# A batch-one attention-and-MLP decode kernel: 128 rows of w2 loaded by five GpSimd loads on chosen partitions, and GpSimd opening the first part

## The chip, the cores and the metric

The kernel runs on one core of a Trainium2 chip. A core has a matmul engine (TensorE, PE in the profile), VectorE (DVE), ScalarE (ACT), GpSimd (POOL) and SyncE (SP), an on-chip memory of 128 partitions (SBUF), accumulators for the matmuls (PSUM), and 16 DMA engines that bring data from HBM. The engines run their own instruction queues and wait for each other by semaphores. A load is issued by an instruction on some engine's queue (here nearly always SP's), cut into packets, and carried by the DMA engines.

The metric is the device time of one execution in microseconds (us). It was measured twice for the kernel before: 400.61 and 400.65, median 400.63. One more execution was taken under the profiler; it has its own time.

## The reference

One token (batch 1, sequence 1) of width 1024 goes through two branches that are added to it:

```python
xn = _layernorm(x)                       # x: [1, 1, 1024]
return x + A_ref(xn, k_cache, v_cache, wq, wo) + B_ref(xn, w1, w2, w3, w4)

# A_ref: q = xn @ wq            wq [1024, 4096], 32 heads of 128
#        scores against k_cache [1, 4, 65536, 128], softmax, times v_cache, 8 query heads per cache head
#        result @ wo            wo [4096, 1024]
# B_ref: h  = gelu(layernorm(xn) @ w1)                    w1 [1024, 1024]
#        hs = concat(four quarters of h, each shifted along the sequence, zeros shifted in) @ w2
#        x1 = xn + hs                                     w2 [1024, 1024]
#        x1 + gelu(layernorm(x1) @ w3) @ w4               w3 [1024, 3584], w4 [3584, 1024]
```

All is bfloat16 in memory. The sequence has length 1, so every shift by one or two places moves zeros in: the row that meets w2 is all zeros whatever h is, and x1 equals xn. The weights and caches together are 169.87 MB, of which the two caches are 134 MB.

## The kernel before

**Staging.** Three large buffers in SBUF (`slot0` to `slot2`, 128 partitions of 64 KB each) take turns. A list called `stream` gives the order: wq, w3, w1 and w2 together ("w12"), then for each of eight units a K tile and a V tile of 8 MB, then wo, then w4. Item n goes to slot n mod 3. Each load spreads its rows over the 128 partitions in order, so that partition m holds the m-th block of rows; a whole slot is 128 rows of 64 KB. w2 is loaded as 8 rows (16 KB) per partition by one load (line 296). All these loads are issued on SP's queue (`prog.load("sp", ...)`, line 89), in the order of the list. When the computation that reads an item has been written, `freed` (line 311) writes down the load of the item three places later; that load waits for the last matmul that reads the slot.

**Recording and waits.** The kernel doesn't call the engines directly. A small layer (`Program`) records every operation with the regions it reads and writes (`region`, line 26), and `plan` (line 124) then works out which operation must wait for which, by overlap of regions. Two operations that touch the same columns on overlapping ranges of partitions are ordered; operations on GpSimd always wait for the GpSimd operation before them (line 151). Each load has a semaphore of its own, raised as it lands. `mm` (line 95) records a matmul and, where the weights at its place in the array aren't those already held, a weight load (LDWEIGHTS). A row times a matrix is done with `row_acc` (line 342): the row's piece, one column of 128 values, is broadcast to 32 columns, and the matmul adds to a 32-partition strip of the accumulator `psB`; strips 0 and 32 take the two 512-wide halves.

**Order.** The load of wq stands in a first part of its own, ahead of everything else (`tile_critical`, line 574, whose opening and closing are done by SP). After it come x_row's load on ACT's queue, w3 and w12 on SP's, and on GpSimd a run of memsets and copies that make constants (lines 325 to 340). Then: the two layer norms; `compute_wq` (q, transposed and written into `qdiag` by GpSimd, line 412); `compute_w3` (gelu, kept in `hT` to the end); `compute_w12` (line 430): 16 matmuls with w1, a gelu, and 16 matmuls of `g_col` with w2, where `g_col` is the row of zeros of the reference. Each of the eight units then transposes its K tile in four DVE instructions, multiplies it with the queries in 64 matmuls (`sc`), finds the maximum, takes the exponential on ACT, transposes the weights on DVE, and multiplies them with V in 64 matmuls (`oacc`). At the end come wo (64 matmuls), and w4 in five loads of 8, 12, 5, 2 and 1 rows per partition (line 19), the last rows in narrow matmuls; two casts and a store by ACT's queue finish.

Of the kernel before, what the change touches and what calls it, by code (L numbers as in the profile page):

```python
# [7 lines left out]
BF16 = mybir.dt.bfloat16  # L8
F32 = mybir.dt.float32
# [5 lines left out]
P = 128  # L15
ROW = 32768
# [3 lines left out]
NARROW = 8  # L20
AHEAD = 5

WIDTH = {F32: 4, BF16: 2}


def region(ap):

    dims, size = list(ap.ap), WIDTH[ap.dtype]
    pitch, rows = dims[0]
    at = ap.offset % pitch  # L30
    last = at + sum((n - 1) * s for s, n in dims[1:])
    p0 = ap.offset // pitch
    return ap.tensor.name, p0, p0 + rows, at * size, (last + 1) * size


def meet(a, b):
    return a[0] == b[0] and a[1] < b[2] and b[1] < a[2] and a[3] < b[4] and b[3] < a[4]


class Op:  # L40
    def __init__(self, engine, emit, reads, writes, alone=False, transfer=False):
        self.engine, self.emit, self.alone, self.transfer = engine, emit, alone, transfer
        self.reads = [region(a) for a in reads]
        self.writes = [region(a) for a in writes]
        self.waits = []
        self.awaited = False


class Program:
# [45 lines left out]
    def mm(self, out, lhsT, rhs, start, stop, pos=(0, 0), size=(P, P)):  # L95

        pe, nc = self.engines["pe"], self.nc
        what = (str(lhsT), size)
        if any(s != size for (_, s), _ in self.held.values()):
            self.held.clear()  # L100
        if pos not in self.held or self.held[pos][0] != what:
            self.add(Op("pe", lambda: pe.ldweights(lhsT, tile_position=pos), [lhsT], []))  # L102
            self.held[pos] = (what, region(lhsT))

        def emit():
            return pe.add_instruction(mybir.InstMatmult(  # L106
                name=nc.get_next_instruction_name(), engine=mybir.EngineType.PE, start_tensor_calc=start,
                stop_tensor_calc=stop, tile_size=size, tile_position=pos, ldweights=False, bass_skip_group_check=True,
                ins=[pe.lower_ap(rhs), pe.lower_ap(lhsT)], outs=[pe.lower_ap(out)]))
        return self.add(Op("pe", emit, [rhs, lhsT], [out]))  # L110
# [13 lines left out]
    def plan(self):  # L124

        known = {e: {} for e in self.engines}
        count = {e: 0 for e in self.engines}
        writers, readers, last_pool = {}, {}, None
        for n, op in enumerate(self.ops):
            e, op.n = op.engine, n  # L130
            need = {}

            def needs(other, raw):
                if other.queue == e and (e in self.IN_ORDER or not raw):
                    return
                if known[e].get(other.queue, 0) < other.at:
                    if other.queue not in need or need[other.queue].at < other.at:
                        need[other.queue] = other

            for r in op.reads:  # L140
                for region_, other in writers.get(r[0], ()):
                    if meet(r, region_):
                        needs(other, True)
            for w in op.writes:
                for region_, other in writers.get(w[0], ()):
                    if meet(w, region_):
                        needs(other, True)
                for region_, other in readers.get(w[0], ()):
                    if meet(w, region_):
                        needs(other, False)  # L150
            if e == "pool" and last_pool is not None:
                needs(last_pool, True)
            picked = sorted(need.values(), key=lambda o: o.n)
            kept = [o for o in picked
                    if not any(o is not x and x.clock.get(o.queue, 0) >= o.at for x in picked)]
            for o in kept:
                o.awaited = True
                for q, at in o.clock.items():
                    known[e][q] = max(known[e].get(q, 0), at)
            op.waits = kept  # L160
            if op.transfer:
                op.queue, op.at = ("dma", n), 1
            else:
                count[e] += 1
                op.queue, op.at = e, count[e]
            if e == "pool":
                last_pool = op
            op.clock = dict(known[e])
            op.clock[op.queue] = op.at
            for w in op.writes:  # L170
                for table in (writers, readers):
                    kept_ = [(r, o) for r, o in table.get(w[0], ())
                             if not (w[1] <= r[1] and r[2] <= w[2] and w[3] <= r[3] and r[4] <= w[4])]
                    table[w[0]] = kept_
                writers[w[0]].append((w, op))
            for r in op.reads:
                readers.setdefault(r[0], []).append((r, op))
# [29 lines left out]
def kernel(  # L207
# [15 lines left out]
    D = A_x.shape[-1]  # L223
# [6 lines left out]
    DC = D // P  # L230
    FC = F // P
    UKEYS = P * ROW // DH
    assert DH == P and HQ // HKV == 8 and HKV == 4 and D == 1024 and F == 3584 and S == 1
    assert SK == 2 * UKEYS and sum(W4_PIECES) == FC
    NB = 2
    NU = HKV * NB
    SCALE = float(DH) ** -0.5
    LEAD = 8 * (SETS - 1)
    COLS = (P, 32)

    prog = Program(nc)
    pe, dve, act, pool = prog, prog.dve, prog.act, prog.pool
# [17 lines left out]
    g_col = sb("g_col", [P, 1], BF16)  # L260
# [14 lines left out]
    sc = ps("sc", [P, SUBS, 512])  # L275
    oacc = ps("oacc", [P, 512])
    pm = [ps(f"pm{i}", [P, 512]) for i in range(2)]
    psB = ps("psB", [P, 512])
# [7 lines left out]
    tiles = {it: slots[i % 3] for i, it in enumerate(stream)}  # L286

    def load(it):
        t = tiles[it]
        if it == "wq":  # L290
            prog.load("sp", t[:], A_wq.rearrange("(p c) n -> p (c n)", c=DC))
        elif it == "w3":
            prog.load("sp", t[:, 0:DC * F], B_w3.rearrange("(p c) f -> p (c f)", c=DC))
        elif it == "w12":
            prog.load("sp", t[:, 0:DC * D], B_w1.rearrange("(p c) n -> p (c n)", c=DC))
            prog.load("sp", t[:, DC * D:2 * DC * D], B_w2.rearrange("(m c) n -> m (c n)", c=DC))
        elif it == "wo":
            prog.load("sp", t[:], A_wo.rearrange("(p j) n -> p (j n)", p=P))
        elif it == "w4":
            w4_v = B_w4.rearrange("(m c) n -> m c n", c=FC)  # L300
            c0 = 0
            for n in W4_PIECES:
                prog.load("sp", t[:, c0 * D:(c0 + n) * D], w4_v[:, c0:c0 + n, :].rearrange("p c n -> p (c n)"))
                c0 += n
        else:
            kind, i = it
            g, b = divmod(i, NB)
            cache = A_k_cache if kind == "K" else A_v_cache
            prog.load("sp", t[:], cache[0, g, b * UKEYS:(b + 1) * UKEYS, :].rearrange("(p ct) d -> p (ct d)", p=P))
# [10 lines left out]
    dve.memset(x_row[:], 0.0)  # L320
    prog.load("act", x_row[0:1, :], A_x[0, 0:1, :])
    load("w3")
    load("w12")

    pool.memset(ident_f[:], 0.0)
    pool.affine_select(out=ident_f[:], in_=ident_f[:], compare_op=ALU.not_equal, fill=1.0, base=0,
# [11 lines left out]
    pool.memset(x_halves[:], 0.0)  # L338
    pool.memset(qdiag[:], 0.0)
    pool.memset(g_col[:], 0.0)  # L340

    def row_acc(j, lhsT, rhs, start=False):
        return pe.mm(psB[32 * j:32 * j + 32, :], lhsT.to_broadcast([P, 32]), rhs, start, False, (0, 32 * j), COLS)

    x_t = p_sb[:, 0:DC * 32].rearrange("p (c j) -> p c j", j=32)
    for a in range(4):
# [29 lines left out]
    _, xn2_rep, _, _ = layernorm(xn, "b")  # L376
# [51 lines left out]
        dve.tensor_copy(out=hT[:], in_=h_row[:, ::32])  # L428

    def compute_w12():  # L430
        wt = tiles["w12"][:, 0:2 * DC * D].rearrange("p (w c n) -> p w c n", w=2, c=DC)
        for c in range(DC):
            for q in range(2):
                pe.mm(sc[0:32, q, :], xn2_rep[:, c, :], wt[:, 0, c, 512 * q:512 * (q + 1)], c == 0, c == DC - 1,
                      (0, 0), COLS)
        h1 = p_sb[0:32, 0:1024].rearrange("p (q n) -> p q n", q=2)
        act.activation(out=h1, in_=sc[0:32, 0:2, :], func=ACTF.Gelu_apprx_tanh)
        for c in range(DC):
            for j in range(2):
                row_acc(j, g_col[:], wt[:, 1, c, 512 * j:512 * (j + 1)], start=(c == 0))  # L440
        freed("w12")

    W = ROW // SETS

    nball = [sb(f"nball{i}", [P, NB]) for i in range(2)]
    lall = [sb(f"lall{i}", [P, NB]) for i in range(2)]
    mx = sb("mx", [P, 1])
    m8 = sb("m8", [1, 8])
    rep = sb("rep", [1, P])
    negmg = sb("negmg", [P, 1])  # L450
    wb = sb("wb", [P, NB])
    lw = sb("lw", [P, NB])
    rl = sb("rl", [P, 1])
# [73 lines left out]
    for u in range(NU):  # L527
        g, b = divmod(u, NB)
# [18 lines left out]
    wt = tiles["w4"]  # L547
# [23 lines left out]
    store = prog.store("act", out[0, 0, :].rearrange("(j n) -> j n", j=2), out_t[31:33].rearrange("p h n -> p (h n)"))  # L571

    prog.plan()
    with tc.tile_critical(sync_engine=mybir.EngineType.SP, no_gpsimd_drain=True):
        prog.emit(0, opening)
    tc.close()
    tc.compile()
# [39 lines left out]
```

## Time and profile before

| | |
|---|---|
| median of the two timed runs | 400.63 us (400.61 to 400.65) |
| the profiled execution, its own time | 400.47 us |
| its span, first to last instruction | 399.2 us |
| busy: PE / DVE / ACT / POOL | 223.5 / 210.2 / 27.6 / 6.2 us |
| loads on SP's and ACT's queues | 3744 packets on SP's, 169.87 MB |
| mean rate over the span | 426 GB/s |
| instructions in the trace: TensorE (with weight loads) | 2250, of 2557 in all |

The page gives busy time and idle time per engine, a picture of the span in 40 slices with the DMA engines' share, the DMA queues with their packets, and a chain: the work that ended last, followed back to what released it. The queues named there are q1 (SP's loads), q10 (ACT's), q8 ("instruction": blocks of 16 KB that the trace shows in 9 packets), and q14 (tables). "SPq" means the queue of SP, which issues a load; a load's duration there is the issue, not the transfer. A load's landing is seen in the trace as 16 marks on its semaphore, and the packets as 16 parallel rows of back-to-back packets; the trace gives packets a queue and times, not the number of their DMA engine.

### The profile page before, as it was taken

How to read it: one execution, taken by the hardware profiler on the slowest of the kernel's cores; microseconds unless marked ns; L12 is line 12 of the kernel's file. 1: busy time of each engine (PE TensorE's matmuls, PEld its weight loads, DVE VectorE, ACT ScalarE, POOL GpSimd, SP SyncE). 2: the span in 40 equal slices, each digit the busy share in tenths (PEclk: the TensorE clock that was granted, in tenths of full speed). 3: DMA queues.
4: the chain of work that ended last, by engine and by line, in shares of the span. 5: the costliest groups of instructions: out<-in, count | busy, mean ns of one | idle time of the engine just before them, and what ended most of it. 6: DMA issues, size and time to landing. Idle time of an engine off the chain costs nothing.

```text
span 399.2 us, 2557 instructions
## 1 busy us (share of the span) xinstructions
PE 223.5 (56%) x1360; PEld 45.8 (11%) x890; DVE 210.2 (53%) x156; ACT 27.6 (7%) x35; POOL 6.2 (2%) x29
## 2 busy tenths in 40 slices
PE   0260970592469256923874196529652946393687
PEld 0210010010100020001001000201020102000233
DVE  0521010975096549653963795259439942793411
ACT  1010030002000200020002000200010011002000
POOL 2000000000000000000000000000000000000000
PEclk9995795598869666978796889568867995698669
DMA  8989999999999999999999999999999999999996
GB/s 329 506 374 419 470 420 427 421 453 479 415 420 427 420 429 427 460 460 420 415 427 420 440 427 455 453 420 420 427 429 440 427 460 435 420 420 427 402 439 259
DMA packets 3760, 170.03 MB, mean 426 GB/s; under 512 B 419, under 2 KB 421, under 8 KB 678
## 3 DMA queue, kind: packets, MB, share of 16 engines
q1 hardware_dynamic: 3744, 169.87, 98.7%
q8 instruction: 9, 0.15, 0.1%
q14 instruction: 1, 0.01, 0.0%
q10 hardware_dynamic: 6, 0.00, 0.0%
HBM read 169.87 MB, written 0.00 MB: 426 GB/s over the span
## 4 chain that ended last, share of the span: by engine, by line
DMA 56%; DVE 24%; PE 14%; another core or an unknown queue 2%; ACT 2%; issue 0%; SPq 0%
DMA slot<-in_A_k_cache_dram 42%; DVE slot L82 19%; PE sc L106 9%; DMA slot<-in_B_w_dram 9%; DMA slot<-in_A_wq_dram 5%; PE oacc L106 4%; DVE p_sb L82 2%; DVE mx L82 2%; ACT p_sb L82 2%; PE pm L122 1%; DVE m L82 0%; DVE rep L82 0%; DVE nball L82 0%; DVE x_halves L82 0%
## 5 line engine op out<-in xcount | busy, mean ns | idle before, releaser
L82 DVE STREAM_TRANSPOSE slot<-slot 128x4096 f32<-128x4096 f32 x32 | 139.4, 4411 | 52.2 <-DMA slot<-in_A_k_cache_dram 52.2
L106 PE MATMUL sc<-slot,qdiag 128*128 128x512 bf16 x512 | 128.2, 410 | 69.0 <-DVE slot L82 68.9
L106 PE MATMUL oacc<-slot,p_sb 128*32 128x512 bf16 x512 | 46.3, 542 | 37.5 <-DVE p_sb L82 18.7
L82 DVE STREAM_TRANSPOSE p_sb<-p_sb 128x2048 bf16<-128x2048 bf16 (+2 forms) x10 | 20.8, 2084 | 38.4 <-ACT p_sb L82 38.3
L82 DVE TENSOR_REDUCE mx<-sc 128x1 f32<-128x2048 f32 x8 | 18.3, 2291 | 29.7 <-PE sc L106 29.7
L102 PEld LDWEIGHTS <-qdiag 128*128 128x128 bf16 x128 | 13.0, 102 | 180.0 <-issue 180.0
L82 ACT ACTIVATE p_sb<-sc,nball 128x2048 bf16<-128x2048 f32 x8 | 15.7, 1967 | 249.9 <-DVE nball L82 249.9
L102 PEld LDWEIGHTS <-p_sb 128*32 128x32 bf16 x512 | 17.3, 131 | 63.3 <-issue 21.8
L106 PE MATMUL sc<-slot,ln_rep_b 128*32 128x512 bf16 (+1 forms) x80 | 16.2, 832 | 8.8 <-DMA slot<-in_B_w_dram 8.6
L82 DVE SCALAR_TENSOR_TENSOR og<-oacc,wb,og 128x512 f32<-128x512 f32 x4 | 3.0, 750 | 19.9 <-PE oacc L106 19.9
L122 PE MATMUL pm<-ident_f,mx 128*1 128x128 f32 x8 | 2.3, 283 | 19.1 <-DVE mx L82 19.1
L106 PE MATMUL psB<-slot,oT 128*32 128x512 bf16 x64 | 9.3, 463 | 1.3 <-DVE oT L82 1.3
L116 PE MATMUL pm<-ol,selx 128*128 128x129 f32 x8 | 2.6, 414 | 10.6 <-DVE ol L82 10.6
L106 PE MATMUL sc<-slot,ln_rep_a 128*32 128x512 bf16 x64 | 6.0, 559 | 4.2 <-DMA slot<-in_A_wq_dram 4.2
L116 PE MATMUL pm<-ln_rowsum_a,msk 128*128 128x1 f32 x2 | 0.6, 363 | 13.5 <-DVE ln_rowsum_a L82 13.5
L82 DVE TENSOR_TENSOR og<-psB,slot 64x512 f32<-64x512 f32 x1 | 0.7, 683 | 13.2 <-PE psB L106 13.2
L82 POOL COPY qdiag<-qx 32x32 bf16<-32x32 bf16 x16 | 3.2, 202 | 277.2 <-PE sc L106 250.5
L82 DVE STREAM_TRANSPOSE p_sb<-x_row 32x256 bf16<-32x256 bf16 x4 | 2.5, 616 | 7.6 <-DMA x_row<-in_A_x_dram 7.6
L122 PE MATMUL pm<-ident_f,rep 1*128 1x1 f32 x8 | 1.9, 235 | 5.0 <-DVE rep L82 5.0
L82 ACT COPY og<-oacc 128x512 f32<-128x512 f32 x4 | 2.3, 585 | 32.9 <-PE oacc L106 32.9
L82 DVE CAST p_sb<-sc 128x512 bf16<-128x512 f32 x1 | 0.7, 691 | 7.4 <-PE sc L106 7.4
L106 PE MATMUL psB<-slot,hT 128*32 128x512 bf16 x40 | 4.5, 379 | 0.0
(86 smaller groups left out, 63.1 us busy)
## 6 DMA issues: line engine op xcount, KB each, us to landing
slot<-in_B_w_dram SPq DMA_DIRECT2D x1, 7168.0 KB, 37.4
slot<-in_B_w_dram SPq DMA_DIRECT2D x3, 2048.0 KB, 43.4
slot<-in_B_w_dram SPq DMA_DIRECT2D x1, 3072.0 KB, 34.5
slot<-in_B_w_dram SPq DMA_DIRECT2D x1, 1280.0 KB, 33.5
slot<-in_B_w_dram SPq DMA_DIRECT2D x1, 512.0 KB, 34.4
slot<-in_B_w_dram SPq DMA_DIRECT2D x1, 256.0 KB, 34.5
slot<-in_A_k_cache_dram SPq DMA_DIRECT2D x8, 42.1
slot<-in_A_v_cache_dram SPq DMA_DIRECT2D x8, 36.9
```

The costliest lines, as they stand in the source:

```text
L82: return program.add(Op(engine, lambda: method(*args, **kw), reads, writes, alone=kw.get("accum_out") is not None))
L102: self.add(Op("pe", lambda: pe.ldweights(lhsT, tile_position=pos), [lhsT], []))
L106: return pe.add_instruction(mybir.InstMatmult(name=nc.get_next_instruction_name(), engine=mybir.EngineType.PE, start_tensor_calc=start, st ...
L116: return self.add(Op("pe", lambda: pe.matmul(out, lhsT=lhsT, rhs=rhs, start=start, stop=stop, tile_position=pos, skip_group_check=True), [ ...
L122: return self.add(Op("pe", lambda: pe.transpose(out, in_, identity), [in_, identity], [out]))
```

## The change

Three things are changed.

- w2's load on SP's queue takes 7 rows per partition instead of 8 (896 rows). The other 128 rows are loaded by five loads on GpSimd's queue, onto 16 chosen partitions: 4 partitions of 17 rows, 2 of 9, 2 of 1, 2 of 17 and 6 of 1. A row is 2 KB. The columns behind the 7 rows are set to zero on partitions 0 to 63 first, by a GpSimd memset of 64 x 8704 float32, since most of them receive fewer than 17 rows. `load("w12")` moves behind GpSimd's memsets in the text.
- `compute_w12` has 14 matmuls over the 7 rows and 34 over the 17 columns of extra rows, the latter on 64 partitions (a tile of 64 x 32).
- The first part is opened and closed by GpSimd instead of SP.

`regions` replaces `region`, so that a load on every fourth partition is known row by row; and a GpSimd load is no longer the operation that the next GpSimd operation waits for.

```diff
+W2_ROWS = 7
+W2_EXTRA = ((0, 4, 4, 17), (1, 4, 2, 9), (2, 4, 2, 1), (16, 4, 2, 17), (24, 4, 6, 1))
...
-def region(ap):
+def regions(ap):
     dims, size = list(ap.ap), WIDTH[ap.dtype]
-    pitch, rows = dims[0]
+    stride, rows = dims[0]
+    pitch = ROW * WIDTH[BF16] // size if ap.tensor.name.startswith("slot") else stride
     at = ap.offset % pitch
     last = at + sum((n - 1) * s for s, n in dims[1:])
     p0 = ap.offset // pitch
-    return ap.tensor.name, p0, p0 + rows, at * size, (last + 1) * size
+    if rows > 1 and stride > pitch:
+        parts = [(p0 + i * (stride // pitch), p0 + i * (stride // pitch) + 1) for i in range(rows)]
+    else:
+        parts = [(p0, p0 + rows)]
+    return [(ap.tensor.name, a, b, at * size, (last + 1) * size) for a, b in parts]
...
-            if e == "pool":
+            if e == "pool" and not op.transfer:
                 last_pool = op
...
-            prog.load("sp", t[:, DC * D:2 * DC * D], B_w2.rearrange("(m c) n -> m (c n)", c=DC))
+            prog.load("sp", t[:, DC * D:W2_REST], B_w2[0:P * W2_ROWS, :].rearrange("(m c) n -> m (c n)", c=W2_ROWS))
+            k0 = P * W2_ROWS
+            for p0, step, k, c in W2_EXTRA:
+                prog.load("pool", t[p0:p0 + step * k:step, W2_REST:W2_REST + c * D],
+                          B_w2[k0:k0 + k * c, :].rearrange("(m c) n -> m (c n)", c=c))
+                k0 += k * c
...
     load("w3")
-    load("w12")
...
     pool.memset(g_col[:], 0.0)
-
-    def row_acc(j, lhsT, rhs, start=False):
-        return pe.mm(psB[32 * j:32 * j + 32, :], lhsT.to_broadcast([P, 32]), rhs, start, False, (0, 32 * j), COLS)
+    more = max(c for _, _, _, c in W2_EXTRA)
+    pool.memset(tiles["w12"][0:64, W2_REST:W2_REST + more * D].bitcast(F32), 0.0)
+    load("w12")
+
+    def row_acc(j, lhsT, rhs, start=False, k=P):
+        return pe.mm(psB[32 * j:32 * j + 32, :], lhsT.to_broadcast([k, 32]), rhs, start, False, (0, 32 * j), (k, 32))
...
-        for c in range(DC):
+        for c in range(W2_ROWS):
             for j in range(2):
-                row_acc(j, g_col[:], wt[:, 1, c, 512 * j:512 * (j + 1)], start=(c == 0))
+                row_acc(j, g_col[:], wt[:, D * (DC + c) + 512 * j:D * (DC + c) + 512 * (j + 1)], start=(c == 0))
+        for c in range(more):
+            for j in range(2):
+                row_acc(j, g_col[0:64, :], wt[0:64, W2_REST + D * c + 512 * j:W2_REST + D * c + 512 * (j + 1)], k=64)
...
-    with tc.tile_critical(sync_engine=mybir.EngineType.SP, no_gpsimd_drain=True):
+    with tc.tile_critical(sync_engine=mybir.EngineType.Pool, no_gpsimd_drain=True):
```

More of the change, by code (lines that the diff above doesn't have):

```diff
@@ L42, in __init__ @@
         self.engine, self.emit, self.alone, self.transfer = engine, emit, alone, transfer
-        self.reads = [region(a) for a in reads]
-        self.writes = [region(a) for a in writes]
+        self.reads = [r for a in reads for r in regions(a)]
+        self.writes = [r for a in writes for r in regions(a)]
         self.waits = []
@@ L102, in mm @@
             self.add(Op("pe", lambda: pe.ldweights(lhsT, tile_position=pos), [lhsT], []))
-            self.held[pos] = (what, region(lhsT))
+            self.held[pos] = (what, regions(lhsT)[0])
         def emit():
@@ L234 @@
     assert SK == 2 * UKEYS and sum(W4_PIECES) == FC
+    W2_REST = (DC + W2_ROWS) * D
     NB = 2
@@ L295, in load @@
             prog.load("sp", t[:, 0:DC * D], B_w1.rearrange("(p c) n -> p (c n)", c=DC))
-            prog.load("sp", t[:, DC * D:2 * DC * D], B_w2.rearrange("(m c) n -> m (c n)", c=DC))
+            prog.load("sp", t[:, DC * D:W2_REST], B_w2[0:P * W2_ROWS, :].rearrange("(m c) n -> m (c n)", c=W2_ROWS))
[4 more added lines that the diff above has]
+                k0 += k * c
+            assert k0 == D
         elif it == "wo":
@@ L430, in compute_w12 @@
     def compute_w12():
-        wt = tiles["w12"][:, 0:2 * DC * D].rearrange("p (w c n) -> p w c n", w=2, c=DC)
+        wt = tiles["w12"]
         for c in range(DC):
             for q in range(2):
-                pe.mm(sc[0:32, q, :], xn2_rep[:, c, :], wt[:, 0, c, 512 * q:512 * (q + 1)], c == 0, c == DC - 1,
+                pe.mm(sc[0:32, q, :], xn2_rep[:, c, :], wt[:, D * c + 512 * q:D * c + 512 * (q + 1)], c == 0, c == DC - 1,
                       (0, 0), COLS)
```

## The prediction

> **What bounds the kernel now.** I read the picture in 40 slices and the table of DMA queues first. The columns of the queue table are packets, MB, and the time the packets took as a share of 16 engines' span.
>
> ```profile
> DMA  8989999999999999999999999999999999999996
> GB/s 329 506 374 419 470 420 427 421 453 479 415 420 427 420 429 427 460 460 420 415 427 420 440 427 455 453 420 420 427 429 440 427 460 435 420 420 427 402 439 259
> q1 hardware_dynamic: 3744, 169.87, 98.7%
> q8 instruction: 9, 0.15, 0.1%
> ```
>
> The DMA engines are busy from the second slice to the last, 98.7% of the span with SP's loads alone, while PE has 56% and DVE 53%. So the time is set by how long 16 DMA engines take for their share, and then by the tail behind the last load. The chain of waits, in order of time, ends so (start, duration, what):
>
> ```profile
> 341.29 17.43 DVE slot L82 x4
> ...
> 362.62 34.50 DMA slot<-in_B_w_dram
> 397.12 0.04 issue
> 397.16 0.34 PE pm L106 x4
> 397.50 0.02 issue
> 397.53 0.43 DVE x_halves L82
> ```
>
> The last w4 load is done at 397.12 and 2.1 us of matmuls, casts and store follow to 399.2. A second path runs close beside it: the last K tile lands at 341.27, and from there DVE and PE work with little pause to 395.13, when the sums with wo and most of w4 end; the narrow matmuls then wait 0.17 and 0.22 us for their loads. So an earlier last load alone gains at most some 0.2 us before PE is late instead (PE is through with what it had at 396.94); only if the last K tile comes earlier as well does the whole end move.
>
> A bulk load ends with its slowest engine. Every load leaves 16 landing marks, one per DMA engine. wq's final packets end within 0.36 us of each other (22.03 to 22.39). The K tile that is in at 127.76 already has a spread of 1.75 us, and from 166 us on it is 1.9 us. Behind the first of the 16, those of w4's first load stand at 0, 0, 0.02, 0.04, 0.07 | 0.30, 0.31 | 0.99 | 1.53, 1.61, 1.63, 1.69, 1.69, 1.70, 1.70, 1.90 us. **Eight engines of sixteen are late by 1.5 us or more.** The trace tells why: the number of late engines rises by one after each q8 packet. The window 396.0 to 397.2 shows one such packet alone (same columns):
>
> ```profile
> q1 hardware_dynamic: 49, 0.08, 17.9%
> q8 instruction: 1, 0.02, 5.5%
> ```
>
> 5.5% of 16 x 1.2 us is 1.05 us for 16 KB, and one engine carries no load meanwhile. After the fetch at 104.44 the next 64 KB packet of that engine also takes 2.89 instead of 2.42 us, so a fetch puts an engine back by 1.05 + 0.47 = some 1.5 us. Eight fetches lie at 43.99, 104.44, 145.74, 198.76, 246.96, 297.93, 338.97 and 377.68, each on another engine; a table load at 75.28 makes the one at 0.99. The ninth, at 396.52, comes too late to hurt. Perfectly even engines would end at the mean of these marks, 0.95 instead of 1.90: about 0.95 us is all that balance can bring.
>
> [...]
>
> **The change part by part.** *Bytes per engine.* The bulk w2 load loses 2 KB on each partition, 8 partitions per engine: 16 KB, by the rate of the 64 KB packets (65,536 B in 2.42 us, 27.1 GB/s) 0.60 us less on every engine. The extra rows come back as 16 shares, one per chosen partition: 17 rows 1.29 us, 9 rows 0.68, 1 row 0.08. If each share has an engine of its own, six engines get 0.68 us more, two 0.08 more, eight 0.53 less. The store, two partitions, shows two packets and x_row, one partition, one packet, so a share per partition is what the trace has for small transfers; it doesn't show on which engine GpSimd's shares come to lie. There are as many light shares (eight) as late engines. With light on late, the late ones come to at most 1.90 - 0.53 = 1.37, the one at 0.99 with a middle share to 1.07, the six fast ones to 0.68 to 0.99: **-0.53 us** at every load from the first K tile on, the last K tile and the last w4 load alike, so both paths move.
>
> *Foreign packets on the engines.* Each engine now carries one GpSimd share between SP's packets. x_row's 2 KB packet on ACT's queue held its engine's next packet back by 0.08 us, which is its bytes: no switching cost. The nearest dear rows are the 16 KB fetch (0.9 us above its bytes) and the 8 KB table load (0.7 above). So 0 to +0.9 us on all 16 alike; I take **+0.1**, nearest to x_row, which like the shares goes from HBM to SBUF.
>
> *The ninth fetch.* PE gains 32 matmuls, 2 weight loads and 2 instructions for waits on five loads; blocks of instructions are therefore used up 36 instructions earlier after w2. The fetches 2 to 8 move by some 1 to 12 us, which changes nothing in their sum. The ninth falls in a dense stretch (80 PE instructions in 4.5 us, 390.65 to 395.13) and comes at about 394.5 to 395.4, while w4's last pieces are still on their way. Its engine loses 1.05 us (packets are small there, so hardly the 0.47). On one that was fast and has a middle share it ends at 0 to 0.31, plus 0.08 and 1.05: 1.13 to 1.44, not far from the 1.28 of the late ones (the last load's slowest mark is 1.81, less 0.53). I take **+0.05** for this.
>
> *GpSimd's queue.* The new memset has 8704 columns; the rows of 536 columns in 0.54 us and of 128 in 0.20 give 1.0 to 1.6 ns each, 8.7 to 14 us. GpSimd is free at 5.57 us, so the memset ends by 14.3 to 19.5, then five issues (SP's take 0.33, ACT's 0.53; even 2 us each would end before 30). The next GpSimd work is the copy of the queries, which began at 31.54, and PE needs that only at 57.8. Cover for either is over 10 us; w2's extra rows are needed by PE at about 57. A share ahead of wq's last packets lets wq land up to 1.3 us later, which moves the wq stage; K's first load was issued at 28.84, while w3 and w12 keep the queue full to 49: hidden. SP's own queue keeps its order, and no load on it waits for GpSimd.
>
> *PE in the w2 stage.* 32 matmuls at 0.21 us (6 in 1.24 on the timeline) are 6.7 us.
>
> ```profile
> 56.64 1.24 PE L106 MATMUL psB<-slot,g_col 128*32 128x512 bf16 x6
> 57.81 0.10 PEld L102 LDWEIGHTS <-qdiag 128*128 128x128 bf16 x1 [1.94 <-issue]
> 57.92 0.33 SPq L89 DMA_DIRECT2D slot<-in_A_k_cache_dram  x1
> 70.17 17.42 DVE L82 STREAM_TRANSPOSE slot<-slot 128x4096 f32<-128x4096 f32 x4 [16.10 <-DMA slot<-in_A_k_cache_dram]
> 74.67 12.61 PE L106 MATMUL sc<-slot,qdiag 128*128 128x512 bf16 x48 [16.79 <-DVE slot L82]
> ```
>
> PE ends at 64.6 instead of 57.9 and is next wanted at 74.67. The K load behind the freed slot is issued at 64.6; the loads ahead of it last to 87.3. Cost 0; cover 10 and 22 us. Were it gone, each us would count in full.
>
> *Opening.* SP's first own instruction was at 0.72 and wq's issue at 0.94, so at most 0.2 us can be gained; waiting for GpSimd's mark, whose next entry is at 0.69, could cost as much. I take 0.
>
> [...]
>
> Sum: -0.53 + 0.10 + 0.05 = -0.38 us, on the profiled execution 400.47 to 400.09. The timed median stands 0.16 above it; 400.63 - 0.38 is **400.25**.
>
> **Rivals.** *(1) The shares fall on the wrong engines.* If heavy shares meet late engines, the slowest becomes 1.90 + 0.68, and the end moves by +0.68: 401.3, slower than before. One such engine of eight is enough. If small loads always begin at the same engine, one engine gets 17 + 9 + 1 + 17 + 1 rows: 92 KB, 3.4 - 0.6 = +2.8 us, 401.6 (a fast engine) to 403.4 (a late one). For it: no view names the engines. Against it: the numbers of shares fit the late and fast groups. *(2) Balance is eaten up.* Switching costs the 0.7 to 0.9 us of the q8 and q14 rows on all engines, or the ninth fetch meets an engine with packets left that is already late (1.28 + 1.05 = 2.33, +0.52): 400.6 to 401.15. It decides from +0.4 of either. *(3) More than balance:* the opening gains its 0.2 and switching costs nothing: 399.9 or a little below.
>
> **How the numbers follow.** Forecast (400.0 to 400.55) 0.55; rival 2, 0.2; rival 1, 0.15, half of it near 401.3; rival 3, 0.1. The range runs from 399.8 to 401.3: it leaves out the far half of rival 1 and a part of 3. A difference of 2% (8 us), about what a measurement of this kernel can tell from no change, is reached by none of the cases; 0.01 for each side is left for what I don't see.
>
> **What would show it.** Right: the marks of a K load's landing late in the run spread about 1.3 us instead of 1.9; the last K tile's transposes start near 340.8, the last w4 load lands near 396.7. Rival 1: a spread above 2.4. Rival 2: spread down, but all loads late by the same amount from about 25 us on, or a q8 packet near 395 with one mark far behind. The opening: wq's issue against 0.94. PE's w2 stage should end near 64.6, idle before the first K tile. The prediction is wrong if DMA stands idle anywhere between 25 and 390 us.

## The result

The changed kernel takes 402.73 us (402.61 and 402.84) against 400.63: a ratio of 1.0054, 95% interval 1.0038 to 1.0071. It is slower, by 2.1 us, and lies outside the range of the prediction, between its forecast (400.25) and the dear end of its first rival (401.6 to 403.4). The profiled execution took 402.84, its span is 401.4 us (before: 400.47 and 399.2).

First the same rows of the page as before: the picture of the DMA engines in 40 slices, and the queues with packets, MB and the time of their packets as a share of 16 engines' span.

```profile
DMA  9999999999999999999999999999999999999994
GB/s 366 451 391 405 454 429 451 445 418 431 426 424 431 464 426 418 431 431 431 439 457 424 418 424 439 438 431 451 424 413 438 444 431 439 438 418 424 405 431 193
q1 hardware_dynamic: 3744, 169.61, 98.1%
q0 software_dynamic: 160, 0.26, 0.2%
q8 instruction: 9, 0.15, 0.1%
```

GpSimd's loads are q0: 0.26 MB moved from one queue to another. The stream has no hole; only the last slice is emptier. The windows say the same (length, then busy time and count per engine, granted clock, DMA share, GB/s), here of the kernel after, behind the first K tile and at the end:

```profile
53.00:390.00 337.00, 200.20 (x1182) 36.77 (x732) 199.49 (x119) 23.37 (x28) 2.43 (x12) 0.79 1.00 432
390.00:401.40 11.40, 8.29 (x94) 3.86 (x90) 1.11 (x2) 0.36 (x1) 0.00 (x0) 0.99 0.54 224
```

and of the kernel before:

```profile
53.00:390.00 337.00, 194.62 (x1137) 37.58 (x732) 199.21 (x119) 22.28 (x26) 2.43 (x12) 0.78 1.00 432
390.00:399.20 9.20, 7.06 (x84) 3.23 (x80) 1.11 (x2) 0.36 (x1) 0.00 (x0) 1.00 0.60 246
```

From 53 to 390 us the engines move 432 GB/s in both. The end is longer, with a lower DMA share: some engines are still working while the others have finished. The chain of waits after, in order of time (start, duration, what), ends as it did:

```profile
343.62 4.46 DVE slot L90
348.08 0.04 issue
348.12 16.62 PE sc L114 x64
...
364.95 34.45 DMA slot<-in_B_w_dram
399.41 0.04 issue
399.45 0.34 PE pm L114 x4
```

The last K tile's transposes begin at 343.62 instead of 341.29 and the last w4 load is in at 399.41 instead of 397.12: both by 2.3 us, and the tail behind is unchanged. So the loss is in the landing of the bulk loads, and it is there long before the end. The 16 landing marks of a load (one per DMA engine, of which the slowest counts) tell where it arises. A mark is sent as a packet of 4 bytes behind the engine's last packet of the load; the times here and below are the starts of these packets, and the semaphore shows the same marks some 0.3 to 0.6 us later. For three loads, first mark, mean and last mark in us:

| load | before: first / mean / last | after: first / mean / last |
|---|---|---|
| wq | 22.03 / 22.16 / 22.39 | 21.98 / 22.52 / 24.01 |
| w3 | 38.95 / 39.08 / 39.31 | 39.12 / 40.15 / 43.66 |
| wo | 377.60 / 378.52 / 379.49 | 377.25 / 379.04 / 381.80 |

At w3 two engines are 4.53 and 4.55 us behind the first, and the next is at 1.69; at wo it is 4.53 and 4.55 against 2.77. **Two engines of 16** set the end, and they have their delay by 43.66 us. The next mark at wo, 380.02 (377.25 + 2.77), is itself 0.5 us later than the last one before, so the two make most of the loss and not all of it.

Which packets did they carry? On one engine a packet begins where the packet before it ended, within some ns, so an engine can be followed. One of the two goes (start, duration, bytes; the bulk packets between them left out): 17.209, 1.288, 34,816; 23.328, 0.686, 18,432; 26.135, 0.084, 2,048; 30.447, 1.972, 34,816; 37.220, 0.084, 2,048. That is a share of every one of the five GpSimd loads: 17 + 9 + 1 + 17 + 1 rows. The other engine has the same. Two more have the 17 and the last 1, two have a 1, and ten have nothing. So the shares didn't get an engine each; each load began at the same engines again.

And the fourth share was slow: 1.972 us where the first, of the same size, took 1.288; the bulk packet behind it took 0.57 more than its 2.12; and a 57 KB bulk packet on a third engine, from 30.462, took 3.358. The same came again at 32.689, with the second share of that load. The bulk packets of most other engines at that time were 0.07 to 0.16 us longer.

### The profile page after: what moved, and what is told of

Same layout as the page of the kernel before. It is cut to its first block, busy times and chain, and to the rows that moved or that the text cites. A ratio compares the mean times of both kernels' runs of the same rounds, so it can differ in the third digit from the quotient of the medians.

```text
span 401.4 us, 2600 instructions
## 1 busy us (share of the span) xinstructions
PE 225.9 (56%) x1392; PEld 45.3 (11%) x892; DVE 210.3 (52%) x156; ACT 27.6 (7%) x35; POOL 16.2 (4%) x35
## 4 chain that ended last, share of the span: by engine, by line
DMA 62%; PE 20%; DVE 15%; ACT 2%; issue 0%; SPq 0%
DMA slot<-in_A_k_cache_dram 43%; DMA slot<-in_B_w_dram 19%; PE sc L114 14%; DVE slot L90 11%; PE oacc L114 4%; DVE p_sb L90 2%; DVE mx L90 2%; ACT p_sb L90 2%; PE psB L114 1%; PE pm L130 0%; DVE m L90 0%; DVE rep L90 0%; DVE nball L90 0%; DVE x_halves L90 0%; PE pm L114 0%
## 5 line engine op out<-in xcount | busy, mean ns | idle before, releaser
L114 PE MATMUL oacc<-slot,p_sb 128*32 128x512 bf16 x512 | 45.4, 532 | 37.5 <-DVE p_sb L90 18.8
L90 ACT ACTIVATE p_sb<-sc,nball 128x2048 bf16<-128x2048 f32 x8 | 15.7, 1967 | 248.4 <-DVE nball L90 248.4
L90 POOL MEMSET slot<- 64x8704 f32 x1 | 7.3, 7344 | 0.1
L114 PE MATMUL psB<-slot,g_col 64*32 64x512 bf16 (+1 forms) x48 | 6.3, 378 | 0.0
```

The costliest lines, as they stand in the source:

```text
L90: return program.add(Op(engine, lambda: method(*args, **kw), reads, writes, alone=kw.get("accum_out") is not None))
L114: return pe.add_instruction(mybir.InstMatmult(name=nc.get_next_instruction_name(), engine=mybir.EngineType.PE, start_tensor_calc=start, st ...
```

## The experiments

The theory after the result is P, for placement: the n-th share of every small load goes to the n-th engine, anew for each load, so two engines carry 45 of the 128 rows; and a share written to partitions that another engine fills in the bulk loads costs more than its bytes. Which partitions an engine fills in the bulk loads no trace here shows: that half of P is the author's assumption, and the partitions of the runs were chosen by it. What a run shows is how long a share took on the partitions it was written to. P's rivals: Q, GpSimd's loads or its opening cost by themselves; P2, partitions from 16 up are slow, whoever writes them.

| run | median us | kernel before beside it | ratio, 95% interval | wo marks: first / mean / last |
|---|---|---|---|---|
| fourth load on 3 and 7 | 401.55 | 400.59 | 1.0023 (1.0013 to 1.0033) | 376.94 / 378.52 / 380.48 |
| opening alone | 400.43 | 400.59 | 0.9995 (0.9986 to 1.0005) | 377.44 / 378.43 / 379.33 |
| one load of 16 x 8 rows | 401.17 | 400.59 | 1.0015 (1.0005 to 1.0024) | 378.10 / 379.23 / 380.42 |
| five loads on SP's queue | 402.75 | 400.59 | 1.0052 (1.0037 to 1.0067) | 377.93 / 379.72 / 381.73 |
| fourth load on 9 and 13 | 402.79 | 400.51 | 1.0056 (1.0043 to 1.0070) | 378.19 / 379.81 / 381.83 |
| fitted, halves | 401.23 | 400.51 | 1.0022 (1.0013 to 1.0031) | 377.50 / 379.02 / 380.24 |
| fitted, halves, SP opens | 401.43 | 400.51 | 1.0020 (1.0012 to 1.0029) | 377.76 / 379.14 / 380.11 |
| fitted, whole pieces | 400.37 | 400.55 | 0.9994 (0.9985 to 1.0003) | 377.40 / 378.66 / 379.35 |

One more, with sixteen small loads, was timed once (401.5, before beside it 400.63). The mean of the 16 marks is worth a column of its own: it is the work of all engines together, and the last mark is what the kernel waits for. The marks are of one execution each, and the mean also holds what differed before any GpSimd load moved: the 64 KB packets that start before 10 us took, per engine, 0.64 us more than 2.42 us each in the run with the opening alone, 0.76 in the kernel before, 0.67 in the changed kernel and up to 0.82 in the others. A difference of 0.2 us between two means is therefore not yet an effect of the edit.

### The fourth load on partitions 3 and 7

```diff
-W2_EXTRA = (..., (16, 4, 2, 17), (24, 4, 6, 1))
+W2_EXTRA = (..., (3, 4, 2, 17), (24, 4, 6, 1))
```

> The fourth GpSimd load (17 rows each) goes to partitions 3 and 7 instead of 16 and 20; nothing else differs from the changed kernel. Theory P (placement): every small load starts at the same lowest engine, so two engines carry 17 + 9 + 1 + 17 + 1 = 45 rows, and the fourth load's shares cost 1.25 us more than their bytes because they are written to partitions that another engine is writing at the same time (its packets there lasted 3.36 instead of 2.12 us). [...] Rival Q: loads on GpSimd's queue, or the opening, cost the time by themselves: 402.7 as before this edit.

401.55, and the shares of 17 rows all take 1.288 us. No bulk packet between 3 and 47 us is lengthened. The two engines are 3.47 and 3.54 behind the first at wo, the same engines with all five shares. P had about 401.5 and holds to 0.05 us, and Q falls: the mean mark, 378.52, is that of the kernel before to the hundredth. Five loads on GpSimd's queue cost the 16 engines no more than some 0.1 us beyond their bytes (the opening alone has 378.43). So the +2.1 has two parts: 0.9 to 1.0 from the stacking of shares on two engines, and 1.2 from where two of them are written. The two engines are not all that stands in the way here: the third-last mark is 2.60 behind the first, at 379.54, no earlier than the last mark before (379.49). Followed back from packet to packet, it is the mark of an engine that has 17 rows and 1 row (17.381 and 34.105) and carries the table load at 76.22 besides: 1.60 behind the first at w3, 2.60 at wo.

### The opening alone

```diff
-    with tc.tile_critical(sync_engine=mybir.EngineType.SP, no_gpsimd_drain=True):
+    with tc.tile_critical(sync_engine=mybir.EngineType.Pool, no_gpsimd_drain=True):
```

> The kernel before, with the first part opened and closed by GpSimd and nothing else. Theory P: wq is issued at 0.89 instead of 0.94 and the rest is as before: 400.58. Rival Q in its form that the opening costs: up to 402.7.

400.43 against 400.59; the interval holds 1, so a gain isn't shown, and a loss of any size that matters is excluded. The first, the mean and the last of its wo marks are 0.16, 0.09 and 0.17 us earlier; its first packets (see above) had already taken 0.13 less.

### Even shares

```diff
-W2_EXTRA = ((0, 4, 4, 17), (1, 4, 2, 9), (2, 4, 2, 1), (16, 4, 2, 17), (24, 4, 6, 1))
+W2_EXTRA = ((0, 4, 16, 8),)
```

> One GpSimd load of 16 partitions with 8 rows each, on partitions 0, 4, ... 60, instead of the five. [...] Rival Q (GpSimd loads cost by themselves, per load): one load instead of five, 401.0; (GpSimd's queue at all): 402.7. [...]

401.17. No two engines stand apart any more (spread at wo 2.32), but all are later: mean 379.23 against 378.43 with the opening alone, 0.8 us in the mean and 0.6 to 1.1 from mark to mark, of which 0.14 lies in the first packets. In the window 14.7 to 15.7 us of this run the thirteen GpSimd packets that start there (0.21 MB) took 64.5% of 16 us, 10.3 us, where their bytes at 27.1 GB/s are 7.9:

```profile
q1 hardware_dynamic: 8, 0.52, 149.8%
q0 software_dynamic: 13, 0.21, 64.5%
```

and all 16 bulk packets of that moment were lengthened, by 0.15 to 0.75 us. The time was at the upper end of what was expected with P (400.7 to 401.2); that the cost fell on all engines was not expected.

### The same five loads on SP's queue

```diff
-                prog.load("pool", t[p0:p0 + step * k:step, W2_REST:W2_REST + c * D],
+                prog.load("sp", t[p0:p0 + step * k:step, W2_REST:W2_REST + c * D],
```

> The same five loads on the same partitions, issued on SP's queue instead of GpSimd's. Theory P: the placement is the same, two engines carry 45 rows; they now stand in one queue with the bulk loads, so two engines write the same partitions at another time and the 1.25 us of the fourth load may or may not come: 401.4 to 402.7. Rival Q: without loads on GpSimd's queue the cost is gone, 400.2 to 400.7.

402.75, as with GpSimd: GpSimd's queue is not needed for the loss, and Q falls again. The last wo mark is the same (381.73 and 381.80), but it is made up otherwise: the two engines are 3.74 and 3.80 behind the first instead of 4.53 and 4.55, and the mean is 0.7 later, so the two times agree to 0.02 us by different sums. Here the two shares of the fourth load went out at the same time (50.19 and 50.26 us), took 2.02 and 2.05 us, and the 64 KB packets of the 14 other engines took 3.40 to 3.67 us instead of 2.42.

### The fourth load on partitions 9 and 13

```diff
-W2_EXTRA = (..., (16, 4, 2, 17), (24, 4, 6, 1))
+W2_EXTRA = (..., (9, 4, 2, 17), (24, 4, 6, 1))
```

> [...] Rival P2 (partitions 16 and up are slow, whoever writes them): 401.5, as with partitions 3 and 7.

402.79, where P had 402.7 with shares of about 2 us: P in time and in the slow shares, and P2 falls. The author expected the bulk packets of two engines alone to be lengthened; those of nearly all engines were. This run and the one on partitions 3 and 7 can be laid side by side, since the shares went out at the same time in both. The window 32.4 to 33.4 us, queues as above; first partitions 3 and 7:

```profile
q1 hardware_dynamic: 12, 0.69, 158.7%
q0 software_dynamic: 14, 0.07, 17.2%
```

then partitions 9 and 13:

```profile
q1 hardware_dynamic: 12, 0.69, 237.4%
q0 software_dynamic: 14, 0.07, 26.6%
```

Same packets, same bytes, two other partitions: GpSimd's packets take 4.26 us instead of 2.75 (26.6% and 17.2% of 16 us), and twelve bulk packets 38.0 instead of 25.4, a good 1 us each. As with SP's queue, two such shares at once slowed nearly all engines; in the changed kernel, where they went out 2.2 us apart, mostly one engine at a time was hit (3.36 and 3.37 us). The trace doesn't number the engines; whether it was the one that fills those partitions is not shown.

### Sixteen small loads

```diff
+W2_EXTRA = tuple((0, 4, k, 1) for k in range(15, 0, -1)) + ((0, 4, 8, 1),)
...
-                prog.load("pool", t[p0:p0 + step * k:step, W2_REST:W2_REST + c * D],
+                prog.load("pool", t[p0:p0 + step * k:step, W2_REST + i * D:W2_REST + (i + 1) * D],
```

> The 128 rows come by sixteen GpSimd loads of one row per partition, on 15, 14, ... 1 and once more 8 partitions (0, 4, 8, ...). Theory P: the n-th partition of every load goes to the n-th engine, so engine 0 carries 16 small packets, engine 1 has 15, down to none on engine 15; the number of 2 KB packets between the bulk packets then names each engine, and from the landing marks one can read which engines the instruction fetches hit. Time 400.6 to 401.2. Rival (the start of a load moves round the engines): the packets spread evenly, 7 to 9 on each.

Followed from packet to packet, the engines have between 2 and 16 small packets; the rival's 7 to 9 on each is not what the trace has. But so many packets end within a few ns of each other that the count of a single engine is not certain, and the engines could not be named one by one as was hoped. The time, 401.5, is above what was expected. The small packets themselves weren't slow (0.08 to 0.10 us), but the 57 KB bulk packets took 2.161 us in the mean instead of 2.116, some 0.36 us per engine (mean mark at wo 379.16); whether the shares on partitions beyond 28 are the cause isn't shown. A load of one single partition was cut into 16 packets of 128 B.

### Shares fitted to the engines

If placement decides, the plan behind the change can be carried out as far as placement allows: more bytes for the engines at which small loads begin, each share on partitions that the author took for its engine's own, fewer bytes for all.

```diff
-W2_EXTRA = ((0, 4, 4, 17), (1, 4, 2, 9), (2, 4, 2, 1), (16, 4, 2, 17), (24, 4, 6, 1))
+W2_EXTRA = ((0, 4, 5, 20), (1, 4, 2, 14))
...
+            prog.load("sp", t[:, DC * D:W2_REST], B_w2.rearrange("(m c) n -> m (c n)", c=DC)[:, 0:DC * D - 512])
...
+                prog.load("pool", t[p0:p0 + step * k:step, W2_REST:W2_REST + r * 512].rearrange("p (r n) -> p r n", n=512),
+                          w2_v[m0:m0 + k * r, DC - 1, 512:1024].rearrange("(k r) n -> k r n", r=r))
```

> The bulk w2 load leaves out the second half of every eighth row (1 KB per partition, 8 KB or 0.30 us per engine). The 128 halves come by two GpSimd loads: 20 halves on each of partitions 0, 4, 8, 12, 16 and 14 more on partitions 1 and 5; GpSimd opens. [...] The late group then comes to 1.60 instead of 1.90: -0.30, and with the opening's -0.16 about 400.15. Rival P2: partition 16 is slow whoever writes it (it was in the slowed load): its share lasts 1.5 instead of 0.8 us and bulk packets beside it lengthen, 400.4 to 401. Rival Q: no gain from bytes, 400.4 or above.

> As the fitted version, but SP opens and closes the first part as in the kernel before. Theory P: -0.30 against the kernel before, 400.3; the difference to the fitted version is the opening alone, 0.05 by the issue of wq and 0.16 by the medians of the run with the opening alone.

401.23 and 401.43: a miss by 1.1 us, for both. A share is no single packet here: its 1 KB runs went out in packets of 4,096 B, with 111 packets of 8 and 16 bytes on the same queue, from 14.7 us on. Bulk packets from 22 to 34 us are lengthened on all engines, mostly by 0.02 to 0.2 us, and the mean mark at wo is 379.02, 0.6 above the run with the opening alone (0.15 of it in the first packets). So the same idea was tried with uncut pieces:

```diff
-W2_EXTRA = ((0, 4, 4, 17), (1, 4, 2, 9), (2, 4, 2, 1), (16, 4, 2, 17), (24, 4, 6, 1))
+W2_EXTRA = ((0, 4, 5, 10), (1, 4, 2, 7))
...
+            prog.load("sp", t[:, DC * D:W2_REST - 512], B_w2[0:k0, :].rearrange("(m c) n -> m (c n)", c=W2_ROWS))
+            prog.load("sp", t[:, W2_REST - 512:W2_REST], B_w2[k0:k0 + P // 2, :].rearrange("r (h n) -> (r h) n", h=2))
```

> As the fitted version (GpSimd opens), but every share is one whole piece of w2: the bulk load takes 7 rows per partition, one more SP load takes 64 rows as 128 halves of 1 KB (one per partition), and the last 64 rows come by two GpSimd loads, 10 rows on each of partitions 0, 4, 8, 12, 16 and 7 more on partitions 1 and 5. In the fitted version with halves the shares went out in packets of 4 KB with small ones of 8 and 16 bytes between, and bulk packets beside them were longer by 0.02 to 0.2 us. Theory P (bytes and own partitions decide; that loss came from the cut-up source): no slowed packet, shares of 0.76 and 0.53 us, the marks' mean at the wo load is again that of the kernel with the opening alone (378.43), and the late group is 0.24 us earlier: 400.2. Rival P3: shares on five engines cost more than their bytes whatever their form, 401 or above; rival P2: partition 16 is slow, 400.5 to 401.

400.37. The shares took 0.761 us on five engines and 0.535 more on two of the five, as their bytes say, no bulk packet beside them was lengthened, and partition 16, written here by the fifth share, was not slow: P on the packets, against P2 and P3. The gain is smaller than forecast: against the kernel before the interval (0.9985 to 1.0003) holds 1, and against the run with the opening alone nothing is left. The last wo mark is at 379.35, 0.14 earlier than before, not 0.24 and the opening's share. The mean mark is 0.23 above that of the opening alone: 0.19 of it stands in the first packets, ahead of GpSimd's loads, and the 1 KB packets of the extra SP load, at 46 ns each, took 0.07 us per engine more than their bytes at 27.1 GB/s. And the end of the chain of waits shows what comes next when the loads get a little earlier:

```profile
381.60 13.81 PE psB L114 x54
395.41 0.02 issue
395.43 0.69 DVE og L90
396.13 0.04 issue
396.17 0.65 PE pm L124 x4
396.82 0.59 PE pm L114 x12
```

It no longer ends in a load: PE is busy from 381.60, and the sums with wo and w4 set the end. No version was found that beats the kernel before beyond its interval.

## Why the prediction was wrong

**The step that failed** is "Bytes per engine": "If each share has an engine of its own, six engines get 0.68 us more, two 0.08 more, eight 0.53 less", and with it "With light on late, the late ones come to at most 1.90 - 0.53". I took the fit of eight light shares to eight late engines as evidence of placement. The trace of before showed only that a small load makes one packet per partition; where a second load would begin was not in it. It began at the same engine, in all five. The sign that the prediction gave for its rival 1, a spread above 2.4, came: 4.55. What stood as the second form of rival 1, at a small chance, is what happened: 45 rows, 3.40 - 0.60 = 2.8 us, "401.6 (a fast engine)". The two were fast engines, and with the fourth load on partitions 3 and 7 the kernel takes 401.55.

**A cost that no step had** is the rest, 1.2 us (402.73 against 401.55): the fourth load's shares on partitions 16 and 20. They took 1.97 and 2.08 instead of 1.29 us and held up bulk packets beside them (3.36 and 3.37 instead of 2.12). For the two engines that set the end: 4.11 us of GpSimd packets and 0.57 on the bulk packet behind, less 0.60, put them at +4.08, and 377.60 + 4.1 is 381.7; the last mark is at 381.80.

**What held.** *Light shares relieve the late engines by 0.53*: in the run on partitions 3 and 7 the seven engines that fetches had put back stand at 378.49 to 378.94 at wo, against 379.13 to 379.50 before, some 0.6 earlier with the earlier start. The gain was there, and hidden behind the two engines with five shares and the one of the table load at 379.54. *Both paths move together*: last K tile and last load, 2.33 and 2.29. *Foreign packets cost what their bytes cost*, on partitions where no share was slow: +0.1 was taken, and at most that was measured (0.09 in the mean mark against the opening alone, 0.08 of it in the first packets). *PE in the w2 stage*: it ends at 65.9, forecast 64.6; the 32 matmuls took 3.6 us instead of 6.7 (45 in 5.65 against 13 in 2.09), but the stage began 4.4 later behind the late w3; DVE's first K transposes start at 72.7, so the cover held. *GpSimd's queue*:

```profile
5.60 7.34 POOL L90 MEMSET slot<- 64x8704 f32 x1
13.24 2.69 POOL L97 DMA_DIRECT2D slot<-in_B_w_dram  x5 [0.30 <-POOL slot L90]
33.03 0.99 POOL L90 COPY qdiag<-qx 32x32 bf16<-32x32 bf16 x4 [17.11 <-DVE qx L90]
```

The memset took 7.34 us (0.84 ns a column, below the 1.0 to 1.6 of the shorter rows) and the five issues 2.69; GpSimd was idle for 17 us after that. *The opening*: wq is issued at 0.89 instead of 0.94, and the first bulk packet starts at 1.88 instead of 1.95.

**What did not come**: the ninth fetch. It was forecast for 394.5 to 395.4 and came at 398.60, as close to the last load as before (0.8 us ahead of 399.41; before 0.6 ahead of 397.12). The +0.05 put down for it is shown by no run; the fetch came 2.1 us later than before instead of 1 to 2 earlier, with no weight for the sum. That 36 more PE instructions bring a fetch earlier was the author's estimate; no run shows it.

**What stays open.** Why two such shares at once slow nearly all 16 engines by about 1 us and one at a time mostly one engine was not found. That the share's place decides is shown: slow on 9 and 13 and on 16 and 20 (1.97 to 2.08 us for 34,816 B), not slow on 3 and 7 (1.288), nor on 16 when the fifth share is written there (0.761 us for 20,480 B). That it is so because another engine fills those partitions is the author's assumption, which no trace shows. Which engine each instruction fetch hits was read for some engines only.

## What to carry to other kernels

In this kernel, bound by its bulk loads, the slowest DMA engines set the end, and the spread of a load's landing marks shows the imbalance at a glance (1.89 us at wo before, 4.55 after); before moving bytes to even it out, run the small loads once and follow their packets, since the fit of counts said nothing about placement here. The five small loads all began at the same engine, so they added up there (45 rows on each of two engines) rather than spread. A share of a small load cost here just its bytes at 27 GB/s of one engine where it was one contiguous piece on partitions 0, 4, 8 and 12 or on 3 and 7 (34,816 B in 1.288 us), and on 16 as a fifth share; on 9 and 13 and on 16 and 20 as the fourth load it took 1.5 to 1.6 times as long, and lengthened the packets of other engines too.

## What was new about the hardware

- Five loads issued by GpSimd, on 4, 2, 2, 2 and 6 partitions, all began at the same DMA engine; a pair of engines had a share of each. SP's queue gave the same time (402.73 and 402.75).
- A 34,816 B packet took 1.288 us on partitions 0, 4, 8 and 12 and on 3 and 7, and 1.97 to 2.08 us on 9 and 13 and on 16 and 20; two at once lengthened the bulk packets of nearly all engines by some 1.0 to 1.2 us.
- Shares made of 1 KB runs went out as 4 KB packets with packets of 8 to 16 bytes beside them, and put the mean mark back by about 0.4 us (0.59 less 0.15 that stands in the first packets), where 128 KB as whole pieces, with one more SP load, put it back by less than 0.1 (0.23 less 0.19).
- In the kernel before, each of the eight 16 KB instruction fetches ahead of 390 us took 1.02 to 1.10 us and put one DMA engine back by about 1.5 us, and up to 390 us it was not made up: the spread of 1.9 us there comes from them.
